# Two transposes of an attention pair in one PSUM tile of two banks, split by one instruction each; value products with one bank

## The chip, the cores and the metric

The kernel runs on one core of a Trainium2 chip. The metric is the device time of one execution in microseconds (us). The engines are TensorE (PE; its weight loads are listed as PEld), VectorE (DVE), ScalarE (ACT), GpSimd (POOL) and SyncE (SP, which here issues DMA). TensorE writes its results into PSUM, eight banks of 512 fp32 values in each partition; ScalarE and VectorE read them from there.

## The reference

Attention whose K and V are averaged over groups of 8 positions feeds two layers of experts. `setup_inputs` multiplies q and k by 8.

```python
# q, k, v: (8, 8, 576, 64) fp32; Sp = 72
k_p = k.reshape(B, H, Sp, 8, D).mean(axis=3)
v_p = v.reshape(B, H, Sp, 8, D).mean(axis=3)
scores = scale * np.matmul(q, k_p.transpose(0, 1, 3, 2))
attn = softmax(scores)                      # over the 72 pooled positions
x = np.matmul(attn, v_p)                    # -> (4608 tokens, 512)
h = np.maximum(np.maximum(x @ w1, x @ w2), x @ w3)      # (4608, 768)
x = h @ w_out                               # (4608, 512)
h = np.maximum(x @ w_in, 0.0)               # (4608, 2048)
out = h * h @ w_out2                        # (4608, 512)
```

## The kernel before

Every fp32 operand of a large product is split in two parts, a high one in the format fp32r and the rest, and a product is three matmuls (high·high, high·low, low·high; `PARTS`). The 4608 tokens are cut into 12 blocks j of `T1` = 384. For each block, attention makes x (512 features as four tiles of 128, one for each pair p of heads), and `moe1(j)` takes x through 18 products with w1, w2, w3 (L528, tile `ps`, evacuated by ScalarE or, as a running maximum `hm`, by VectorE at L536) and four with w_out (L547). The last layer, `moe2`, uses combinations of blocks of its operands and begins at 753 us. Its weights are prepared during the first stage.

`attend` makes the six steps of one pair in one piece of a block; a piece lies within one batch and has n = 384 or 192 tokens. `load` issues K (`kr`, 128x576), q (`qr`) and V (`vr`, 72x1024) on SyncE's queue. `prepare` sums K over groups of 8 on VectorE (L240, `ks`) and writes the scaled result on ScalarE (`kbd`). `softmax` sums V (L247, `vs`), splits it (`vst`), and makes scores (L362, tile `sc`), row maxima (L364, `st`), exponentials (L367), sums and reciprocals (L371, L372), and on GpSimd the normalisation (`ss`). From j = 2 on, `carry` copies the result by DMA into the format that a faster transpose takes (`ssr`). `transpose` turns each head's part on TensorE (L395, `tr`), and ScalarE and VectorE split it (L399 and L400, `pt`). `values` multiplies by V (L424, L425, `av`), joins the two halves of the head (L427 on ScalarE, L428 on VectorE, tile `xf`), and splits the joined tile into x (L134 on ScalarE, L135 on VectorE). Batch 0 is handled "whole": its weights are not split, and its V is pooled by a matmul.

64 pairs of a piece and a pair of heads are computed: 8 whole, 56 split, of these 28 with n = 384 and 28 with 192.

A `kr` buffer and a `vr` buffer are handed out by `place`, by turns: first from four places that the raw weights use too, and after the last weight of w_out has been asked for, from two, so that the loads of K then follow one another in one place and those of V in the other. Raw weights of 8 bytes an element come as `wraw` on SyncE, are rebuilt as fp32 by ScalarE (L161, L162) and VectorE (L163, L166, `wbits`), and split into `w` by ScalarE (L134) and GpSimd (L135).

Every step enters a list with a due time and is emitted in that order; the framework's scheduler then orders the instructions of each engine by its own model of their times. PSUM holds three banks for `ps`, two for `sc`, one for `tr` and two for `av0` and `av1`; the transpose of the second head borrows `av1`.

Of the kernel before, what the change touches and what calls it, by code (L numbers as in the profile page):

```python
# [10 lines left out]
F32 = mybir.dt.float32  # L11
F32R = mybir.dt.float32r
I32 = mybir.dt.int32
U32 = mybir.dt.uint32
AF = mybir.ActivationFunctionType
ALU = mybir.AluOpType
# [4 lines left out]
P = 128  # L21
B, H, S, D = 8, 8, 576, 64
POOL = 8
SP = S // POOL
# [9 lines left out]
T1 = 384  # L34
# [50 lines left out]
def as_f32(ap):  # L85
    return ap.bitcast(F32)
# [8 lines left out]
def attention_moe_kernel(ctx: ExitStack, tc: tile.TileContext, q, k, v, vn, w1, w2, w3, wo1, wi2, wo2, out):  # L95
    nc = tc.nc
# [6 lines left out]
    ident = const.tile([P, P], F32R, name="ident")  # L103
# [4 lines left out]
    for sign, base in ((1, POOL * MID), (-1, POOL - 1 - POOL * MID)):  # L108
        nc.gpsimd.affine_select(
            out=sums, in_=sums, compare_op=ALU.is_ge, fill=0.0, base=base,  # L110
# [22 lines left out]
    def split_to(hi, lo, src, engine):  # L133
        nc.scalar.activation(hi, src, AF.Copy)  # L134
        engine.tensor_tensor(out=lo, in0=src, in1=as_f32(hi), op=ALU.subtract)  # L135

    def split(hl, src, engine=nc.vector):

        split_to(hl[:, 0], hl[:, 1], src, engine)
# [53 lines left out]
    tr_ps = s_at.enter_context(tc.tile_pool(name="tr_ps", bufs=1, space=PSUM))  # L193
    av_ps = s_at.enter_context(tc.tile_pool(name="av_ps", bufs=1, space=PSUM))
# [93 lines left out]
    def score_tiles(n):  # L288
        m = P if n % P == 0 else n // 2
        return [(c, m) for c in range(0, n, m)]  # L290
# [37 lines left out]
    def attend(j, b, s0, n, p, t):  # L328

        kr, vr, qr, pt, sms = [], [], [], [], []  # L330
        first, whole, carried = s0 == 0, b < NATURAL, j >= CARRIED
# [19 lines left out]
        tiles = score_tiles(n)  # L351
        m = tiles[0][1]
# [29 lines left out]
            sms[0] = ssr  # L382

        def transpose():
            if whole:
                pt.append(pt_p.tile([SP, 2, T1], F32, tag="pt", name="pt"))
            else:
                pt.append(pt_p.tile([SP, 2, 2, T1], F32R, tag="pt", name="pt"))
            for h in range(2):
                if h:  # L390
                    tr = av_ps.tile([P, T1], F32R if carried else F32, tag="av1", name="tr")[:SP, :n]
                else:
                    tr = tr_ps.tile([SP, T1], F32R if carried else F32, tag="tr", name="tr")[:, :n]
                for i, (c, _) in enumerate(tiles):
                    nc.tensor.transpose(tr[:, c : c + m], sms[0][:, i, h], (ident if carried else as_f32(ident))[:m, :m])  # L395
                tr = as_f32(tr) if carried else tr
                if not whole:
                    hi, lo = pt[0][:, 0, h, :n], pt[0][:, 1, h, :n]
                    nc.scalar.activation(hi, tr, AF.Copy)  # L399
                    nc.vector.tensor_tensor(out=lo, in0=tr, in1=as_f32(hi), op=ALU.subtract)  # L400
                elif h:
                    nc.vector.tensor_copy(pt[0][:, h, :n], tr)
                else:
                    nc.scalar.activation(pt[0][:, h, :n], tr, AF.Copy)

        def values():
            if t == 0:
                x_t[j][p] = x_p.tile([P, 2, T1], F32R, tag="x", name="x")
            x = x_t[j][p][:, :, t : t + n]
            if whole:  # L410
                av = av_ps.tile([P, T1], F32, tag="av0", name="av0")[:, :n]
                for h in range(2):
                    nc.tensor.matmul(
                        av, lhsT=vst_f[p // 2][:, p % 2, h : h + 2].rearrange("p a d -> p (a d)"), rhs=pt[0][:, h, :n],
                        start=(h == 0), stop=(h == 1),
                    )
                split(x, av)
                return
            hi, lo = pt[0][:, 0, :, :n], pt[0][:, 1, :, :n]
            xf = xf_p.tile([P, T1], F32, tag="xf", name="xf")[:, :n]  # L420
            for h in range(2):
                av = av_ps.tile([P, T1], F32, tag=f"av{h}", name=f"av{h}")[:, :n]
                lhsT = vst[:, p, 2 * h : 2 * h + 2].rearrange("p a d -> p (a d)")
                nc.tensor.matmul(av, lhsT=lhsT, rhs=hi[:, h], start=True, stop=False)  # L424
                nc.tensor.matmul(av, lhsT=lhsT, rhs=lo[:, h], start=False, stop=True)  # L425
                r, o = slice(h * D, (h + 1) * D), slice((1 - h) * D, (2 - h) * D)
                nc.scalar.activation(xf[r], av[o], AF.Copy)  # L427
                nc.vector.tensor_tensor(out=xf[r], in0=av[r], in1=xf[r], op=ALU.add)  # L428
            split(x, xf)

        return load, prepare, softmax, carry, transpose, values

    w1_t, wo1_t = {}, {}
# [395 lines left out]
    for j in range(NB2):  # L829
        for gr in range(NG):  # L830
            more = j + 1 < NB2
            c = moe2_in(j, gr)
# [55 lines left out]
```

## Time and profile before

| | before |
|---|---|
| median of three runs | 1465.66 us (1464.34 to 1467.58) |
| profiled execution | 1463.68 us |
| its span, first to last instruction | 1462.0 us |
| busy: PE, DVE, ACT, POOL | 1426.7, 983.3, 762.5, 177.5 us |
| mean granted TensorE clock | 0.993 of full |

The time of an execution holds the span and about 1.7 us around it. Busy time is the time in which an engine ran an instruction; consecutive instructions of an engine can overlap a little in the records.

### The profile page before, as it was taken

The page shows a single profiled execution, that of the slowest core. Times are in us where ns is not written, and L with a number is a line of the kernel's source. Part 1 is how long each engine was busy: PE and PEld are TensorE (multiplying, and loading weights), DVE is VectorE, ACT ScalarE, POOL GpSimd, SP SyncE. Part 2 cuts the span into 40 slices and gives each one's busy share as a digit, 9 for nine tenths or more (in the row PEclk, how much of TensorE's full clock was granted, in tenths as well). Part 3 has the DMA queues.
Part 4 walks back from the last instruction along what each step waited for, and adds up shares of the span by engine and source line. Part 5 has one row for each costly group of instructions (what it writes and reads, how often), then busy time and mean ns, then how long its engine had stood idle before and what let it go on. Part 6 is the DMA issues. An engine that isn't in the chain of part 4 may idle for free.

```text
span 1462.0 us, 27667 instructions
## 1 busy us (share of the span) xinstructions
PE 1426.7 (98%) x10410; PEld 1401.6 (96%) x10410; DVE 983.3 (67%) x1778; ACT 762.5 (52%) x1983; POOL 177.5 (12%) x229
## 2 busy tenths in 40 slices
PE   6889999999999999999999999999999999999998
PEld 4879999999999999999999999999999999999998
DVE  5896476766765856756336768686766768686775
ACT  7795366664666656654323545363534445454443
POOL 3441022311312212221000000000000000000000
PEclk9999999999999999999999999999999999999999
DMA  7654145543455544432549857666567665665746
GB/s 226 188 164 140 62 145 181 173 137 130 145 170 187 151 145 144 127 123 86 187 162 356 280 176 240 220 208 217 214 231 230 229 212 213 205 238 179 277 139 229
DMA packets 125029, 272.81 MB, mean 187 GB/s; under 512 B 13504, under 2 KB 69568, under 8 KB 124896
## 3 DMA queue, kind: packets, MB, share of 16 engines
q1 hardware_dynamic: 117984, 261.61, 53.4%
q10 hardware_dynamic: 6912, 9.44, 1.8%
q8 instruction: 82, 1.34, 0.4%
q14 instruction: 51, 0.42, 0.1%
HBM read 213.91 MB, written 48.23 MB: 179 GB/s over the span
## 4 chain that ended last, share of the span: by engine, by line
PE 89%; DMA 6%; ACT 3%; DVE 2%; issue 1%; SPq 0%; POOL 0%; DVEq 0%; ACTq 0%; POOLq 0%
PE ps L528 29%; PE ps L688 23%; PE ps L547 10%; PE accB L812 6%; PE accA L812 6%; PE accF L812 3%; DMA wo2s<-wo_dram 3%; PE accE L812 3%; PE accD L812 2%; PE sc L362 2%; ACT ss L367 1%; PE tr L395 1%; PE av L425 1%; PE av L424 1%; DMA kq<-in_k_dram 1%
## 5 line engine op out<-in xcount | busy, mean ns | idle before, releaser
L528 PE MATMUL ps<-x,w 128*128 128x384 f32 x2592 | 493.8, 341 | 5.3 <-ACT w L134 2.7
L528 PEld LDWEIGHTS ps<-x,w 128*128 128x128 f32 x2592 | 449.6, 189 | 8.5 <-ACT w L134 3.0
L688 PE MATMUL ps<-y,wi2s 128*128 128x256 f32 x3024 | 371.5, 277 | 0.5 <-DVE c L659 0.2
L688 PEld LDWEIGHTS ps<-y,wi2s 128*128 128x128 f32 x3024 | 356.6, 188 | 1.5 <-DVE a L659 0.7
L547 PE MATMUL ps<-h,wo 128*128 128x384 f32 x864 | 162.2, 339 | 0.1
L547 PEld LDWEIGHTS ps<-h,wo 128*128 128x128 f32 x864 | 149.2, 188 | 0.7 <-POOL wo L135 0.4
L701 ACT ACTIVATE c<-c 128x512 f32<-128x512 f32 x90 | 56.3, 627 | 169.7 <-DVE c L659 169.1
L659 DVE TENSOR_TENSOR c<-ps,c 128x512 f32<-128x512 f32 x144 | 98.2, 687 | 67.3 <-PE ps L688 64.4
L536 DVE TENSOR_TENSOR hm<-ps,hm 128x384 f32<-128x384 f32 x144 | 79.6, 552 | 76.6 <-PE ps L528 73.6
L134 ACT ACTIVATE g<-c 128x512 fp32r<-128x512 f32 x144 | 90.3, 627 | 56.9 <-DVE c L698 23.3
L812 PE MATMUL accA<-wo2s,g 128*128 128x256 f32 x864 | 115.7, 277 | 0.0
L812 PE MATMUL accB<-wo2s,g 128*128 128x256 f32 x864 | 111.1, 277 | 4.5 <-DMA wo2s<-wo_dram 3.5
L812 PEld LDWEIGHTS accB<-wo2s,g 128*128 128x128 f32 x864 | 104.0, 188 | 5.7 <-issue 1.9
L135 DVE TENSOR_TENSOR g<-c,g 128x512 fp32r<-128x512 f32 x144 | 97.8, 685 | 16.5 <-ACT g L134 16.4
L812 PEld LDWEIGHTS accA<-wo2s,g 128*128 128x128 f32 x864 | 107.1, 188 | 0.0
L367 ACT ACTIVATE ss<-sc,st 128x72 f32<-128x72 f32 (+1 forms) x320 | 98.0, 321 | 15.0 <-DVE st L364 12.0
L373 POOL TENSOR_TENSOR ss<-ss,st 128x432 f32<-128x432 f32 (+1 forms) x64 | 53.7, 839 | 238.8 <-DVE st L372 96.4
L400 DVE TENSOR_TENSOR pt<-tr,pt 72x192 fp32r<-72x192 f32 (+1 forms) x112 | 48.8, 448 | 46.5 <-ACT pt L399 44.9
L427 ACT ACTIVATE xf<-av 64x192 f32<-64x192 f32 (+1 forms) x112 | 45.4, 405 | 58.8 <-PE av L425 47.5
L428 DVE TENSOR_TENSOR xf<-av,xf 64x192 f32<-64x192 f32 (+1 forms) x112 | 50.8, 453 | 36.7 <-ACT xf L427 34.8
L134 ACT ACTIVATE h<-hm 128x384 fp32r<-128x384 f32 x72 | 37.6, 522 | 57.1 <-DVE hm L536 56.4
L367 ACT ACTIVATION_READ_ACCUMULATOR ss<-sc,st 128x1 f32 (+1 forms) x320 | 66.3, 207 | 0.0
(107 smaller groups left out, 1936.5 us busy)
## 6 DMA issues: line engine op xcount, KB each, us to landing
wo2s<-wo_dram SPq DMA_DIRECT2D x252, 512.0 KB
wi2s<-wi_dram SPq DMA_DIRECT2D x24, 512.0 KB
wraw<-in_wo_dram SPq DMA_DIRECT2D x22, 512.0 KB
wraw<-in_w_dram SPq DMA_DIRECT2D x18, 512.0 KB
y_dram<-ys ACTq DMA_DIRECT2D x48, 192.0 KB
wraw<-in_wi_dram SPq DMA_DIRECT2D x16, 512.0 KB
wi_dram<-wraw SPq DMA_DIRECT2D x16, 512.0 KB
wo_dram<-wraw SPq DMA_DIRECT2D x64, 128.0 KB
```

The source lines that it names most:

```text
L134: nc.scalar.activation(hi, src, AF.Copy)
L135: engine.tensor_tensor(out=lo, in0=src, in1=as_f32(hi), op=ALU.subtract)
L367: nc.scalar.activation(ss[:, i, h], src[:, i, h], AF.Exp, bias=st[:, 0, i, h : h + 1], accum_out=st[:, 1, i, h : h + 1],)
L373: nc.gpsimd.tensor_tensor(out=ss, in0=ss, in1=st[:, 2].rearrange("p g (h o) -> p g h o", o=1).to_broadcast([m, g, 2, SP]), op=ALU.mult,)
L428: nc.vector.tensor_tensor(out=xf[r], in0=av[r], in1=xf[r], op=ALU.add)
L528: nc.tensor.matmul(ps, lhsT=w1_t[f, e][:, a, kk * P : (kk + 1) * P], rhs=x[kk][:, c], start=(n == 0), stop=(n == 3 * KD - 1),)
L536: nc.vector.tensor_tensor(out=hm, in0=ps, in1=hm, op=ALU.max)
L547: nc.tensor.matmul(ps, lhsT=wo1_t[kk][:, a, d * P : (d + 1) * P], rhs=hs[kk][:, c], start=(n == 0), stop=(n == 3 * KF1 - 1),)
L659: nc.vector.tensor_tensor(out=out, in0=in0, in1=in1, op=ALU.add)
L688: nc.tensor.matmul(bank[:, u * HT : (u + 1) * HT], lhsT=wi2_t[2 * gr + u][i][:, a, o + kk * P : o + (kk + 1) * P], rhs=y_t[j][m][:, c, kk] ...
L701: nc.scalar.activation(c, c, AF.Relu)
L812: nc.tensor.matmul(bank[:, i * 256 : (i + 1) * 256], lhsT=g[:, a, u * HT + i * P : u * HT + (i + 1) * P], rhs=w[:, u, c], start=(n == 0 an ...
```

## The change

Both heads are transposed into one tile of two banks, one bank for each head, and the tile is split by one ScalarE and one VectorE instruction for the two heads (in `split_to`, so at L134 and L135). The bank that this takes comes from the value products: they have one bank instead of two. For n = 192 the two heads use different halves of it. The transpose of the second head no longer borrows a value bank.

```diff
         def transpose():
+            kind = F32R if carried else F32
+            tr = tr_ps.tile([SP, 2, 512], kind, tag="tr", name="tr")[:, :, :n]
+            for h in range(2):
+                for i, (c, _) in enumerate(tiles):
+                    nc.tensor.transpose(
+                        tr[:, h, c : c + m], sms[0][:, i, h], (ident if carried else as_f32(ident))[:m, :m]
+                    )
+            tr = as_f32(tr) if carried else tr
             if whole:
                 pt.append(pt_p.tile([SP, 2, T1], F32, tag="pt", name="pt"))
+                nc.scalar.activation(pt[0][:, 0, :n], tr[:, 0], AF.Copy)
+                nc.vector.tensor_copy(pt[0][:, 1, :n], tr[:, 1])
             else:
                 pt.append(pt_p.tile([SP, 2, 2, T1], F32R, tag="pt", name="pt"))
-            for h in range(2):
-                if h:
-                    tr = av_ps.tile([P, T1], F32R if carried else F32, tag="av1", name="tr")[:SP, :n]
-                else:
-                    tr = tr_ps.tile([SP, T1], F32R if carried else F32, tag="tr", name="tr")[:, :n]
-                for i, (c, _) in enumerate(tiles):
-                    nc.tensor.transpose(tr[:, c : c + m], sms[0][:, i, h], (ident if carried else as_f32(ident))[:m, :m])
-                tr = as_f32(tr) if carried else tr
-                if not whole:
-                    hi, lo = pt[0][:, 0, h, :n], pt[0][:, 1, h, :n]
-                    nc.scalar.activation(hi, tr, AF.Copy)
-                    nc.vector.tensor_tensor(out=lo, in0=tr, in1=as_f32(hi), op=ALU.subtract)
-                elif h:
-                    nc.vector.tensor_copy(pt[0][:, h, :n], tr)
-                else:
-                    nc.scalar.activation(pt[0][:, h, :n], tr, AF.Copy)
+                split_to(pt[0][:, 0, :, :n], pt[0][:, 1, :, :n], tr, nc.vector)
...
-                av = av_ps.tile([P, T1], F32, tag="av0", name="av0")[:, :n]
+                av = av_ps.tile([P, 512], F32, tag="av", name="av")[:, :n]
...
+            both = av_ps.tile([P, 512], F32, tag="av", name="av") if 2 * n <= 512 else None
             for h in range(2):
-                av = av_ps.tile([P, T1], F32, tag=f"av{h}", name=f"av{h}")[:, :n]
+                if both is None:
+                    av = av_ps.tile([P, 512], F32, tag="av", name="av")[:, :n]
+                else:
+                    av = both[:, h * n : (h + 1) * n]
```

The scheduler puts other instructions in another order too, most in the first 130 us. On VectorE, at the place where x of the last pair of block 1 is finished, the order before reads as follows; the first row is that x, the ks and vs behind it belong to the K and V of batch 2:

```order
L135 TENSOR_TENSOR x<-xf,x 128x192
L166 SCALAR_TENSOR_TENSOR wbits<-wraw,wbits 128x512
L247 TENSOR_REDUCE vs<-vr 72x128
L400 TENSOR_TENSOR pt<-tr,pt 72x384
L163 SCALAR_TENSOR_TENSOR wbits<-wbits,wraw 128x512
L428 TENSOR_TENSOR xf<-av_1460,xf 64x384
L536 TENSOR_TENSOR hm<-ps,hm 128x384
L240 TENSOR_REDUCE ks<-kr 128x72
L400 TENSOR_TENSOR pt<-tr,pt 72x384
L166 SCALAR_TENSOR_TENSOR wbits<-wraw,wbits 128x512
```

The same place on VectorE after the change, line numbers shifted by one (L427 is the old L428); the x of the last pair is the third row from the end:

```order
L247 TENSOR_REDUCE vs<-vr 72x128
L364 TENSOR_REDUCE st<-sc 128x6
L240 TENSOR_REDUCE ks<-kr 128x72
L427 TENSOR_TENSOR xf<-av,xf 64x192
L371 TENSOR_SCALAR st<-st 128x6
L372 RECIPROCAL st<-st 128x6
L240 TENSOR_REDUCE ks<-kr 128x72
L427 TENSOR_TENSOR xf<-av,xf 64x192
L135 TENSOR_TENSOR pt<-tr,pt 72x768
L135 TENSOR_TENSOR x<-xf,x 128x192
L240 TENSOR_REDUCE ks<-kr 128x72
L364 TENSOR_REDUCE st<-sc 128x6
```

Two vs and three ks (one of each stands a little ahead of the rows shown) have moved ahead of the x of the last pair; the last wbits rows, which stood behind it, stand ahead of it too.

On TensorE the order after the change reads as follows between two blocks, about a fifth of the way through the program; av is the value bank, and the rows of 192 and of 384 columns belong to two pieces:

```order
L362 MATMUL sc<-kbd,qr 128x144 x3
L423 MATMUL av<-pt,vst 128x192
L424 MATMUL av<-pt,vst 128x192
L362 MATMUL sc<-kbd,qr 128x144 x3
L423 MATMUL av<-pt,vst 128x384
L424 MATMUL av<-pt,vst 128x384
L389 MATMUL tr<-ident,ssr 72x128 x6
L362 MATMUL sc<-kbd,qr 128x144 x3
```

The transposes of both heads stand together in one row of six, where before they stood in two rows of three, and only three score matmuls stand here between one use of the value bank and the next.

## Rows read from the trace of the kernel before

**Rows 1.** The page, part 1: busy us, share of the span, instructions.

```profile
PE 1426.7 (98%) x10410; PEld 1401.6 (96%) x10410; DVE 983.3 (67%) x1778; ACT 762.5 (52%) x1983; POOL 177.5 (12%) x229
```

**Rows 2.** Stretches: length, busy us (instructions) of each engine, clock, DMA share, GB/s.

```profile
0.00:20.00 20.00, 12.69 (x49) 7.17 (x50) 6.96 (x14) 10.39 (x47) 4.65 (x15) 1.00 0.79 256
20.00:40.00 20.00, 14.72 (x69) 11.59 (x66) 16.17 (x32) 18.09 (x71) 8.33 (x7) 0.83 0.64 185
...
80.00:100.00 20.00, 16.95 (x93) 15.64 (x92) 18.59 (x35) 18.63 (x66) 9.71 (x8) 0.93 0.53 164
100.00:150.00 50.00, 49.05 (x288) 48.08 (x288) 35.18 (x63) 28.42 (x82) 11.47 (x10) 0.97 0.42 123
150.00:200.00 50.00, 50.00 (x303) 49.82 (x302) 23.72 (x44) 21.17 (x61) 4.24 (x8) 1.00 0.26 82
```

**Rows 3.** TensorE's timeline: start, duration, operation, [idle before it <- releaser].

```profile
98.73 0.63 PE L528 MATMUL ps<-x,w 128*128 128x384 f32 x2 [1.88 <-ACT w L134]
...
110.09 0.97 PE L528 MATMUL ps<-x,w 128*128 128x384 f32 x4 [0.85 <-DVE x L135]
```

**Rows 4.** Groups by shape, pt: count, busy us, mean ns, idle before.

```profile
L399 ACT ACTIVATE pt<-tr 72x384 fp32r<-72x384 f32 x56 | 25.5, 481 | 12.2 <-PE tr L395 11.5 <-ACT ys L553 0.4
...
L399 ACT ACTIVATE pt<-tr 72x192 fp32r<-72x192 f32 x56 | 17.4, 320 | 7.8 <-PE tr L395 7.2 <-ACT pt L399 0.4
...
L400 DVE TENSOR_TENSOR pt<-tr,pt 72x384 fp32r<-72x384 f32 x56 | 29.8, 548 | 37.9 <-ACT pt L399 37.1
...
L400 DVE TENSOR_TENSOR pt<-tr,pt 72x192 fp32r<-72x192 f32 x56 | 19.1, 349 | 8.6 <-ACT pt L399 7.8
```

**Rows 5.** TensorE's timeline, 157 to 180 us.

```profile
157.93 0.53 PE L395 MATMUL tr<-ident,ssr 128*72 128x128 f32 x6
158.29 2.33 PE L528 MATMUL ps<-x,w 128*128 128x384 f32 x12
...
163.60 10.28 PE L547 MATMUL ps<-h,wo 128*128 128x384 f32 x58
...
178.66 0.90 PE L362 MATMUL sc<-kbd,qr 128*128 128x144 f32 x6
```

**Rows 6.** Groups by shape, xf, 384 columns.

```profile
L427 ACT ACTIVATE xf<-av 64x384 f32<-64x384 f32 x56 | 27.2, 486 | 29.7 <-PE av L425 28.4
...
L428 DVE TENSOR_TENSOR xf<-av,xf 64x384 f32<-64x384 f32 x56 | 31.0, 553 | 18.1 <-ACT xf L427 17.1
```

**Rows 7.** TensorE's timeline between two blocks.

```profile
302.12 0.41 PE L424 MATMUL av<-pt,vst 72*128 72x384 f32 x1 [0.48 <-DVE pt L400]
```

**Rows 8.** VectorE's timeline, 109 to 132 us.

```profile
109.09 0.68 DVE L166 SCALAR_TENSOR_TENSOR wbits<-wraw,wbits 128x512 int32<-128x512 int32 x1
109.69 0.34 DVE L135 TENSOR_TENSOR x<-xf,x 128x192 fp32r<-128x192 f32 x1
...
115.79 1.22 DVE L247 TENSOR_REDUCE vs<-vr 72x128 f32<-72x1024 f32 x1 [0.20 <-DMA vr<-in_v_dram]
...
122.01 0.75 DVE L240 TENSOR_REDUCE ks<-kr 128x72 f32<-128x576 f32 x1 [1.99 <-DMA kr<-in_k_dram]
...
131.59 0.75 DVE L240 TENSOR_REDUCE ks<-kr 128x72 f32<-128x576 f32 x1 [3.13 <-DMA kr<-in_k_dram]
```

**Rows 9.** SyncE's DMA queue, timeline: time of issue.

```profile
111.79 0.32 SPq L235 DMA_DIRECT2D vr<-in_v_dram  x1
...
118.33 0.34 SPq L230 DMA_DIRECT2D kr<-in_k_dram  x1
```

**Rows 10.** Groups by shape, VectorE reductions.

```profile
L247 DVE TENSOR_REDUCE vs<-vr 72x128 f32<-72x1024 f32 x28 | 33.9, 1211 | 4.2 <-DMA vr<-in_v_dram 3.9
...
L240 DVE TENSOR_REDUCE ks<-kr 128x72 f32<-128x576 f32 x28 | 20.8, 744 | 12.1 <-DMA kr<-in_k_dram 10.0 <-ACT kbd L243 1.8
...
L364 DVE TENSOR_REDUCE st<-sc 128x6 f32<-128x432 f32 x32 | 19.1, 598 | 13.5 <-PE sc L362 13.3
```

**Rows 11.** VectorE's timeline, a wait for a weight conversion.

```profile
102.78 1.35 DVE L163 SCALAR_TENSOR_TENSOR wbits<-wbits,wraw 128x512 int32<-128x512 int32 x1 [1.76 <-ACT wbits L161]
```

## The prediction

> **What bounds the kernel now.** I read the page first. TensorE is busy for 98% of the span, VectorE for 67%, ScalarE for 52% [rows 1]. So an instruction taken from ScalarE or VectorE is worth nothing by itself; it counts only where TensorE waits for those engines. 1462.0 − 1426.7 leaves 35.3 us in which TensorE does nothing, and the table of stretches says where: it lacks 7.3 us up to 20, 5.3 in 20 to 40, 3.1 in 80 to 100, then 0.95 up to 150, and nothing up to 200 [rows 2]. In the second and third of these stretches VectorE and ScalarE are busy 81 to 93%: the start-up, in which weights are rebuilt, K and V pooled and two blocks of attention run, is the only place where they set the pace. TensorE's own timeline then names the last two gates: 1.88 us at 98.73 for a split weight, 0.85 us at 110.09 for the low half of x of pair 3 of block 1 [rows 3]. From there TensorE's chain has no wait until 299. The profiled execution took 1463.7 us, 2.0 less than the median of the runs; the sum below is made on it and then moved up by 2.0.
>
> **What is removed, and its price.** 56 pairs are split; each loses one ScalarE and one VectorE instruction. Rows price the old ones: ScalarE 320 ns for 192 columns and 481 for 384, VectorE 349 and 548 [rows 4]. Twice 192 columns in one instruction should cost about what 384 cost now, so ScalarE saves 2·320 − 481 = 159 ns and VectorE 2·349 − 548 = 150 ns. For 768 columns I extend the line by 161 and 199 ns per 192 columns: 803 and 946 ns, again 159 and 150 saved. Over 56 pairs this is 8.9 us of ScalarE and 8.4 of VectorE. After 100 us both have 30% or more to spare [rows 2], so of it only the merged pairs ahead of the gates can count: by the order four of 192 columns and two of 384, 0.9 us per engine. On TensorE the transposes are the same number in fewer runs: it changes from one kind of matmul to another 815 times in the program before and 762 after. A run of 12 costs 2.24 − 0.08 of overlap = 2.16 us where 58 cost 10.28, 0.177 each [rows 5], so 12 cost 2.12 and a change of kind about 0.04. 53 × 0.04 = 2.1 us if each change costs it; only 15 of the 53 are on the long runs of products, which gives 0.6. I take 0.8 as gain, between 0 and 2.1.
>
> **What the single value bank adds.** The second head's products must now wait until the first head's xf copy and add have read the bank. That takes one ScalarE and one VectorE row: 486 + 553 ns for 384 columns [rows 6], about 1.1 us with the hand-overs, and less for 192. Counting the order of TensorE after the change, 2 us or more of other matmuls stand between the two heads at all but four of the 56 places; those four, at three block boundaries and in the start-up, have 0, 0.3, 0.3 and 0.9 us (0.3 is three score matmuls, as between the value products in the part of TensorE's order shown). There I put in 0.7, 0.7 and 0.5 less what was lost there before: the first boundary already waits 0.48 for the like, a pt row [rows 7]. Net +1.0, bounded by 0 (the waits replace one another) and 3.4 (three full 1.1).
> The Trainium skill ("PSUM — Partial Sum Buffer", section "PSUM bank collisions raise a hardware error") speaks against the change here: a bank which one engine reads may not be written by another, at other columns either, so that halves of one bank are no two buffers and the 192-column tile "both" gains no overlap over the wider one. By it every one of the 56 pairs pays, and the sum would be rival C's. The order, which shows the wait at 192 columns too, agrees with the rule; what hides it is the work between.
>
> **What moves: VectorE's queue in the start-up.** The two orders are the largest change. VectorE takes its queue in order, and a reduction of K (ks) or V (vs) at its head holds all behind it until the load lands. Loads of kr share one buffer and those of vr another, and SyncE issues one only when the reduction before has read it: kr issued at 118.33 was reduced at 122.01, 3.7 us later; vr 111.79 to 115.79, 4.0 [rows 8, 9]. So two ks with less than 3.7 us of VectorE work between stall. Before, such stalls of 1.99 and 3.13 us stand at 122.01 and 131.59 [rows 8], behind the x of pair 3, and TensorE, with x in hand, does not wait. After, three ks and two vs stand ahead of that x.
> First the work. Ahead of x of pair 3 the order after holds on VectorE 3 ks, 2 vs, 3 wbits and 3 st rows more, and for pt 4 rows of 2 × 192 columns and 2 of 768 in place of 8 of 192 and one of 384. By start-to-start times (a row's duration less the 0.08 by which the next starts early): ks 3·0.67, vs 2·1.13, wbits 3·0.60, st 0.7 (one reduction of 0.52, two short rows), pt 4·0.47 + 2·0.87 − 8·0.27 − 0.47 = 1.0; together 7.8 us [rows 4, 8, 10]. On TensorE the same point stands behind 28 more products, 9 scores and 6 transposes: 28·0.177 + 9·0.11 + 6·0.06 = 6.3 us [rows 5]. The gate had no slack (0.85 us of wait), so this alone is +1.5. At the x of pair 2 it is 7 wbits, a ks, a vs, an h and an hm: +7.0 of VectorE against +2.7 of TensorE, less a slack of about half a us, +3.8, which the later gate contains.
> Then the stalls. In the rows of VectorE's order after, xf, st and a reciprocal stand between the first ks shown and the second, 0.28 + 0.07 + 0.10 = 0.45 us against 3.7: a stall of 3.3. Between the vs shown first and the one before it stand 3.3 us (2 wbits, 2 of 192 columns, a ks and a pt of 768) against 4.0: 0.7. Together +4.0; nothing if the loads come earlier than I think, 5.1 if the first of them waits as well.
> Against it: VectorE waits for ScalarE's conversions before this gate, 1.76 us at 102.78 the longest [rows 11]; with more to do it will find more of them ready. I take back 1.5, of 4.4 that the waits from 70 us on come to.
> Behind the gate the next two ks (1.4 and 1.5 us of work ahead of them since the last, so stalls of 2.3 and 2.2) delay the xf which frees the value bank and the hm which frees a product bank, with 3.5 and 7.7 us of TensorE work as cover against 4.0 and 8.4 of VectorE: +1.4.
>
> **Sum.** 1.5 + 4.0 − 1.5 + 1.4 (start-up) + 1.0 (boundaries) − 0.8 (runs) = +5.6 us, 1469.3 on the profiled execution, 1471 against the median. All terms at their kind ends: 1.5 + 0 − 4.4 + 0 + 0 − 2.1 = −5.0; at the unkind: 1.5 + 5.1 − 0 + 2.5 + 3.4 − 0 = +12.5, with 2.5 for both late hand-overs in full.
>
> **Rivals.** A, no change: the ks stalls are there but land on TensorE work, as those before do, or the loads arrive early; then 1.5 − 1.5 + 1.0 − 0.8 = 0.2: 1465.9. For it speaks that the start-up has many orders of the same length; against it that 0.45 us between two ks cannot hide 3.7. B, faster: the start-up is bound by ScalarE's conversions, not by x. The last split of a weight (1.88 us of wait at 98.73) has about 3 us less of ScalarE work ahead of it in the order after, by my count of its rows; if that gate goes (−1.9), VectorE gains its 0.9 on the x gate, and 0.8 comes from the runs: 1465.7 − 3.6 = 1462. It decides if no ks stall over 1 us falls before x of pair 3. C, the bank: were there no work between the two heads, 56 × 1.1 = 62 us, 1527; the order excludes nearly all of it, and 2 of 56 places more than I count cost 2 us, which the range holds. D, the clock: it was granted at 0.83 of full at 20 to 40 us, where TensorE idled, 0.93 at 80 to 100 and 1.00 at 150 to 200 [rows 2], so mostly at 2.4 GHz with parts at 1.2. New idle near 115 could bring a part of 1.2 GHz there: my guess is 2 to 4 us more, 1473 to 1475.
>
> **How the numbers follow.** Forecast with its waits at 1468.6 to 1476: 0.53. A: 0.20. B: 0.13. D: 0.12. C in a visible size: 0.02. A measurement here tells 0.2%, 2.9 us, from no change. Faster than 1462.7: B, 0.12. Same: A, a little of B and the lower edge of the forecast, 0.24. Slower: 0.64. The range leaves out the last tenth of B and of D: 1461.5 to 1477.5; the forecast's own is 1468 to 1475.
>
> **What would show it.** In the profile after, VectorE idle before L240 for the kr load, 2 to 3 us at a time, between 110 and 130 us; TensorE waiting there for VectorE's x or xf, with its busy time in 100 to 150 down from 49.05 to about 44. 28 pt rows each of about 481 and 803 ns on ScalarE. Waits of under 1 us for xf at three block boundaries. From 150 on the same distances as before. I am wrong if TensorE's start-up idle stays at 20 us (A), if it shrinks (B), or if value products wait for xf at many of the pairs (C).

## The result and the profile after

The change makes the kernel slower: 1483.81 us median of five runs (1479.77 to 1484.51) against 1465.66 (1464.34 to 1468.41), a ratio of 1.0122 with a 95% interval of 1.0108 to 1.0136. The direction was forecast, the size was not: +18 us against +5.6, outside the range. The profiled execution has a span of 1482.0 us, 20.0 more than that of [rows 1].

The page of the changed kernel, part 1:

```profile
PE 1437.1 (97%) x10410; PEld 1408.6 (95%) x10410; DVE 974.8 (66%) x1722; ACT 756.7 (51%) x1927; POOL 180.6 (12%) x229
```

VectorE and ScalarE have 56 instructions fewer each and 8.5 and 5.8 us less to do. TensorE has the same 10410 matmuls. It is idle for 1482.0 − 1437.1 = 44.9 us, 9.6 more than in [rows 1], and busy for 10.4 us more with the same work. In this execution a lower clock accounts for some 9 of these 10.4: its mean went from 0.993 to 0.987 of full, and 0.013·1482 − 0.007·1462 = 9.0. That share holds for this execution alone. The five executions of the changed kernel had mean clocks of 0.987, 0.992, 0.990, 0.993 and 0.991, and the one at 0.993 took 1482.44 us all the same; by their mean of 0.991 the clock would account for some 3 us. What the other executions lost in its place is not shown.

The merged instructions, groups by shape (count, busy us, mean ns, idle before); they answer to [rows 4]:

```profile
L134 ACT ACTIVATE pt<-tr 72x768 fp32r<-72x768 f32 x28 | 22.5, 805 | 10.8 <-PE tr L389 10.4
...
L134 ACT ACTIVATE pt<-tr 72x384 fp32r<-72x384 f32 x28 | 13.6, 484 | 2.3 <-PE tr L389 1.8
...
L135 DVE TENSOR_TENSOR pt<-tr,pt 72x768 fp32r<-72x768 f32 x28 | 26.7, 952 | 29.7 <-ACT pt L134 29.6
...
L135 DVE TENSOR_TENSOR pt<-tr,pt 72x384 fp32r<-72x384 f32 x28 | 15.5, 552 | 2.8 <-ACT pt L134 1.7
```

They cost what was forecast (803 and 481, 946 and 548 ns). The saving is real and lies beside TensorE's work.

To see where the time went I cut both executions at the same pieces of work, by counting the products of `moe1` (L528 and L547 before, L527 and L546 after): the starts of the 433rd, 1081st, 1405th, 1981st, 2269th, 2809th and 3241st. Stretches of the kernel before, columns as in [rows 2]:

```profile
0.00:147.13 147.13, 125.85 (x673) 111.57 (x673) 109.10 (x209) 105.64 (x364) 52.38 (x55) 0.93 0.58 178
147.13:277.27 130.14, 130.14 (x801) 129.10 (x801) 79.90 (x172) 71.37 (x234) 24.43 (x36) 1.00 0.41 132
277.27:346.46 69.19, 68.01 (x419) 66.68 (x419) 46.80 (x94) 42.74 (x146) 16.86 (x24) 1.00 0.50 162
...
462.80:521.09 58.29, 58.29 (x360) 57.86 (x358) 39.98 (x78) 36.44 (x114) 15.92 (x21) 1.00 0.52 168
...
630.36:715.70 85.34, 84.40 (x504) 82.67 (x503) 42.49 (x84) 40.61 (x111) 15.90 (x21) 1.00 0.45 146
```

The same stretches of the changed kernel:

```profile
0.00:157.36 157.36, 130.94 (x685) 113.16 (x686) 109.96 (x205) 107.51 (x368) 54.28 (x56) 0.93 0.54 168
157.36:285.66 128.30, 128.30 (x789) 127.57 (x789) 77.07 (x159) 70.63 (x223) 24.28 (x36) 1.00 0.41 131
285.66:360.80 75.14, 71.47 (x425) 70.01 (x425) 48.46 (x95) 45.19 (x149) 19.21 (x27) 0.95 0.49 158
...
475.54:540.70 65.16, 63.94 (x390) 62.91 (x390) 43.37 (x89) 42.82 (x152) 18.68 (x24) 0.97 0.51 164
...
646.51:734.30 87.79, 85.57 (x508) 84.57 (x508) 44.50 (x86) 42.81 (x112) 16.25 (x21) 0.98 0.43 146
```

The start-up is 10.2 us longer (157.36 against 147.13). The three stretches that hold a change of block with many scores are longer by 5.9, 6.9 and 2.5, and there the clock, 1.00 before, has a mean of 0.95, 0.97 and 0.98. The stretches between are shorter by 1.8, 1.6 and 3.5, in part because some attention work has moved into their neighbours: the three longer ones hold 6, 30 and 4 more matmuls, the start-up 12 more. Up to the 3241st product this adds up to 10.2 + 8.4 = 18.6 us; the last layer adds 1.4.

The 8.4 us are clearer when the part from the 433rd to the 3241st product is taken whole, before and after:

```profile
147.13:715.70 568.57, 566.45 (x3476) 559.69 (x3475) 357.96 (x751) 327.98 (x1053) 125.14 (x174) 1.00 0.46 145
```

```profile
157.36:734.30 576.94, 569.56 (x3464) 563.61 (x3464) 349.90 (x702) 321.49 (x994) 126.29 (x173) 0.99 0.44 143
```

TensorE's idle time there goes from 2.1 to 7.4 us, 5.3 more. The clock stands at half in three places near 313, 494 and 671 us, 13.6 us in all, which costs 6.8. Of these 12.1 only 8.4 show, because TensorE's other work takes 3.7 us less. 12 score matmuls have moved into the start-up (1.3 us at 0.11 each). The remaining 2.4 fit the fewer changes from one kind of matmul to another: counted in TensorE's order there are 363 in this part, 414 before, and 51 of them at the prediction's 0.04 are 2.0.

How a boundary is lost is seen best at 668 us, in three timelines of the changed kernel (start, duration, operation, [idle before it <- releaser]). TensorE:

```profile
668.22 0.35 PE L423 MATMUL av<-pt,vst 72*128 72x192 f32 x1
668.41 0.27 PE L424 MATMUL av<-pt,vst 72*128 72x192 f32 x1
670.90 0.45 PE L423 MATMUL av<-pt,vst 72*128 72x384 f32 x1 [2.22 <-DVE xf L427]
```

ScalarE and VectorE in the same stretch:

```profile
667.80 0.32 ACT L367 ACTIVATE ss<-sc,st 128x72 f32<-128x72 f32 x1
...
669.59 0.35 ACT L367 ACTIVATE ss<-sc,st 128x72 f32<-128x72 f32 x1
...
670.05 0.32 ACT L426 ACTIVATE xf<-av 64x192 f32<-64x192 f32 x1
```

```profile
670.49 0.36 DVE L427 TENSOR_TENSOR xf<-av,xf 64x192 f32<-64x192 f32 x1
```

The products of a pair's second head are written by 668.7, and the first head of the next pair needs their bank. The copy that begins to free the bank stands behind four more exponentials in ScalarE's queue and starts at 670.05; VectorE's add ends at 670.85, and TensorE goes on at 670.90. Two short instructions (0.32 and 0.36) make a hand-over of 2.2 us, because ScalarE takes its queue in order. The Trainium skill says so of these engines ("PSUM — Partial Sum Buffer", section "Engine vs sequencer instructions": their queues are strictly first in, first out); this trace agrees, with 1.4 us for which the copy stood ready. Of the six waits for xf ahead of value products in this execution three are of this kind, from one pair to the next (1.10, 0.56 and 2.22 us); in the other three the second head waits for the first (0.97, 1.11 and 0.27).

At the boundary near 310 us there are three waits of the kind (1.11 and 0.56 for xf, 1.00 for pt), and then the clock falls. TensorE's timeline there, six products before and nine after:

```profile
307.21 1.30 PE L527 MATMUL ps<-x,w 128*128 128x384 f32 x6
...
315.83 3.26 PE L527 MATMUL ps<-x,w 128*128 128x384 f32 x9
```

The nine take 0.36 us each, where the six before took 0.22 with their ends: the granted level went from 2.4 to 1.2 GHz, with the work that follows the waits. Two stretches of the changed kernel at half clock, this one and one in the start-up:

```profile
312.90:319.70 6.80, 5.89 (x24) 5.85 (x25) 3.32 (x9) 3.99 (x22) 1.03 (x2) 0.50 0.17 57
...
111.50:118.30 6.80, 6.19 (x25) 6.14 (x26) 5.26 (x8) 3.04 (x14) 3.11 (x3) 0.50 0.37 108
```

The start-up, TensorE's timeline of the changed kernel from 102 to 125 us:

```profile
102.86 0.35 PE L423 MATMUL av<-pt,vst 72*128 72x192 f32 x1 [1.10 <-DVE xf L427]
...
108.65 0.36 PE L423 MATMUL av<-pt,vst 72*128 72x192 f32 x1 [0.97 <-DVE xf L427]
...
112.11 1.33 PE L546 MATMUL ps<-h,wo 128*128 128x384 f32 x3 [2.45 <-POOL wo L135]
...
123.69 0.44 PE L423 MATMUL av<-pt,vst 72*128 72x384 f32 x1
...
124.78 0.61 PE L527 MATMUL ps<-x,w 128*128 128x384 f32 x2
```

VectorE, same kernel, the K reductions that I had forecast as stalls:

```profile
122.48 0.75 DVE L240 TENSOR_REDUCE ks<-kr 128x72 f32<-128x576 f32 x1 [2.32 <-DMA kr<-in_k_dram]
...
126.16 0.75 DVE L240 TENSOR_REDUCE ks<-kr 128x72 f32<-128x576 f32 x1 [1.28 <-DMA kr<-in_k_dram]
```

The stalls are there. But TensorE is late before them, through hand-overs of the bank and a weight split on GpSimd: it starts the 246th product at 116.70 us, 6.6 later than before, and the first stall begins at 120.16. It reaches the x of pair 3 (124.53 on VectorE, 124.78 on TensorE) without an idle time; from 113 to 129 us its one wait is 0.38 at 119.48, for ScalarE.

### The profile page after: what moved, and what is told of

Its sections match the earlier page's. It is cut to its first block, busy times and chain, and to the rows that moved or that the text cites. A ratio compares the mean times of both kernels' runs of the same rounds, so it can differ in the third digit from the quotient of the medians.

```text
span 1482.0 us, 27649 instructions
## 1 busy us (share of the span) xinstructions
PE 1437.1 (97%) x10410; PEld 1408.6 (95%) x10410; DVE 974.8 (66%) x1722; ACT 756.7 (51%) x1927; POOL 180.6 (12%) x229
## 4 chain that ended last, share of the span: by engine, by line
PE 79%; DMA 10%; DVE 4%; ACT 3%; issue 2%; POOL 1%; SPq 0%; ACTq 0%; POOLq 0%; DVEq 0%
PE ps L527 25%; PE ps L687 21%; PE ps L546 8%; PE accB L811 6%; PE accA L811 6%; DMA wo2s<-wo_dram 5%; PE accE L811 3%; PE accF L811 3%; PE accD L811 2%; PE sc L362 2%; DMA kr<-in_k_dram 1%; ACT ss L367 1%; PE tr L389 1%; PE av L423 1%; DMA wraw<-in_wi_dram 1%
## 5 line engine op out<-in xcount | busy, mean ns | idle before, releaser
L527 PE MATMUL ps<-x,w 128*128 128x384 f32 x2592 | 497.2, 342 | 5.8 <-POOL w L135 1.8
L527 PEld LDWEIGHTS ps<-x,w 128*128 128x128 f32 x2592 | 452.8, 190 | 10.2 <-POOL w L135 2.8
L546 PE MATMUL ps<-h,wo 128*128 128x384 f32 x864 | 162.3, 339 | 3.8 <-POOL wo L135 3.0
L546 PEld LDWEIGHTS ps<-h,wo 128*128 128x128 f32 x864 | 150.2, 189 | 5.3 <-POOL wo L135 3.9
L134 ACT ACTIVATE g<-c 128x512 fp32r<-128x512 f32 x144 | 90.3, 627 | 58.9 <-DVE c L697 23.3
L135 DVE TENSOR_TENSOR g<-c,g 128x512 fp32r<-128x512 f32 x144 | 97.6, 685 | 17.3 <-ACT g L134 17.3
L427 DVE TENSOR_TENSOR xf<-av,xf 64x192 f32<-64x192 f32 (+1 forms) x112 | 50.8, 454 | 59.5 <-ACT xf L426 58.2
L134 ACT ACTIVATE h<-hm 128x384 fp32r<-128x384 f32 x72 | 37.6, 522 | 59.3 <-DVE hm L535 59.1
L135 DVE TENSOR_TENSOR pt<-tr,pt 72x384 fp32r<-72x384 f32 (+1 forms) x56 | 42.1, 752 | 32.6 <-ACT pt L134 31.3
```

What stands on the lines that cost most here:

```text
L527: nc.tensor.matmul(ps, lhsT=w1_t[f, e][:, a, kk * P : (kk + 1) * P], rhs=x[kk][:, c], start=(n == 0), stop=(n == 3 * KD - 1),)
L546: nc.tensor.matmul(ps, lhsT=wo1_t[kk][:, a, d * P : (d + 1) * P], rhs=hs[kk][:, c], start=(n == 0), stop=(n == 3 * KF1 - 1),)
```

## The experiments

The theory "bank" or "hand-over": what costs is that the value products wait for the evacuation of the one bank, the second head's for the first head's and the next pair's for the second head's, behind what stands in the two queues, and the clock behind the waits. Its rivals: "order" (any such change puts the start-up in a worse order) and "K stall", the theory of the prediction. "Late at 432" below is the start of the 433rd product of `moe1` less 147.13, that of the kernel before; "later part" is what is added between it and the 3241st product. Both come from one profiled execution of each kernel. Executions of one kernel differ by several us (19 of the kernel before: 1462.61 to 1470.13), so 2 or 3 us between two such numbers say little. The changed kernel has 10.2 and +8.4.

**Merge without losing a bank** (e1), on the kernel before, for 192 columns alone:

```diff
+            if n <= 256 and not whole:
+                tr = tr_ps.tile([SP, T1], kind, tag="tr", name="tr")[:, : 2 * n].rearrange("s (h n) -> s h n", h=2)
...
+                split_to(pt[0][:, 0, :, :n], pt[0][:, 1, :, :n], tr, nc.vector)
+                return
```

> Merges the two heads' transposes and their split for the 28 pairs of 192 columns alone, into the one transpose bank; the two value banks stay. Theory 'bank' (the single value bank costs the time, through waits for xf and the lower clock behind them): no loss, 1462 to 1467 us. Theory 'order' (any merge puts the start-up in a worse order on VectorE, K and V reductions ahead of x, and that is 8 of the 18 us): 1471 to 1476 us, with TensorE busy for about 43 of the 50 us from 100 to 150.

Measured: 1468.27 us, ratio 1.0009 (0.9993 to 1.0024). Late at 432: 3.1; later part −2.6. That is just above the range of "bank" and well below that of "order". A merge at 192 columns that takes no bank away costs nothing that can be measured, and gains nothing either; the wide pairs were not merged without the loss of a bank. "Order" as stated, that any merge costs 8 us in the start-up, falls.

**One bank without the merge** (e2), on the kernel before:

```diff
-    tr_ps = s_at.enter_context(tc.tile_pool(name="tr_ps", bufs=1, space=PSUM))
+    tr_ps = s_at.enter_context(tc.tile_pool(name="tr_ps", bufs=2, space=PSUM))
...
-                    tr = av_ps.tile([P, T1], F32R if carried else F32, tag="av1", name="tr")[:SP, :n]
+                    tr = tr_ps.tile([SP, T1], F32R if carried else F32, tag="tr", name="tr")[:, :n]
...
+            both = av_ps.tile([P, 512], F32, tag="av", name="av") if 2 * n <= 512 else None
             for h in range(2):
-                av = av_ps.tile([P, T1], F32, tag=f"av{h}", name=f"av{h}")[:, :n]
+                if both is None:
+                    av = av_ps.tile([P, 512], F32, tag="av", name="av")[:, :n]
+                else:
+                    av = both[:, h * n : (h + 1) * n]
```

> Nothing is merged: each head is transposed into a bank of its own, two banks that take turns, and split by its own instructions; the value products have one bank as in the change. Theory 'bank': the whole loss is there without any merge, 1480 to 1486 us, waits of TensorE for xf at block boundaries near 300, 490 and 670 us. Theory 'order' (the merge does the start-up's part): 1472 to 1477 us.

Measured: 1486.24 us, ratio 1.0124 (1.0090 to 1.0157). Late at 432: 12.0; later part +6.2. The whole loss is there with nothing merged, as "bank" said, 0.2 us above its range.

**Products of both heads first** (e3), on the changed kernel:

```diff
+            if both is not None:
+                multiply(0)
+                multiply(1)
             for h in range(2):
+                if both is None:
+                    multiply(h)
...
                 nc.scalar.activation(xf[r], av[o], AF.Copy)
```

> The change, but for 192 columns the products of both heads are written before the first copy out of the bank, so the second head has no wait for the first. Theory 'bank': about half of the hand-overs are gone, 1472 to 1477 us, and the waits for xf in front of 192-column products are gone. Theory 'order': the start-up keeps its loss, and with it 1478 to 1484 us.

Measured: 1469.10 us, ratio 1.0020 (1.0008 to 1.0032). Late at 432: 6.3; later part −4.9. This gives back 15 of the 18 us, more than the 7 to 12 that I expected. TensorE's timeline of this kernel shows the four matmuls of a pair in one go:

```profile
285.08 0.26 PE L425 MATMUL av<-pt,vst 72*128 72x192 f32 x1
285.17 0.27 PE L426 MATMUL av<-pt,vst 72*128 72x192 f32 x1
285.28 0.27 PE L425 MATMUL av<-pt,vst 72*128 72x192 f32 x1
285.39 0.27 PE L426 MATMUL av<-pt,vst 72*128 72x192 f32 x1
```

What TensorE waits for ahead of the value products, from the list of waits (waited for, us in total, times, longest us), of the kernel before, of the changed kernel, of e2 and of e3:

```profile
PE av L424 <- DVE xf L428: 0.9, 1, 0.9
```

```profile
PE av L423 <- DVE xf L427: 6.2, 6, 2.2
```

```profile
PE av L428 <- DVE xf L432: 4.6, 5, 1.8
```

```profile
PE av L425 <- DVE xf L438: 2.1, 4, 0.9
```

The Trainium skill's rule that the prediction cites ("PSUM — Partial Sum Buffer", section "PSUM bank collisions raise a hardware error": no two engines on one bank at once in the same partitions, at other columns either) is kept here by the program's waits: in the traces of the changed kernel and of e3 none of the 224 value products runs while xf reads a value bank, where in the kernel before, with two banks, 20 do. Written first, both halves are done before any reading begins, and the rule costs nothing within a pair; the four waits that e3 has left are from one pair to the next.

**The bank taken from the scores** (e4): the changed kernel with `sc_ps` of one bank and `av_ps` of two.

```diff
-    sc_ps = s_at.enter_context(tc.tile_pool(name="sc_ps", bufs=2, space=PSUM))
+    sc_ps = s_at.enter_context(tc.tile_pool(name="sc_ps", bufs=1, space=PSUM))
...
-    av_ps = s_at.enter_context(tc.tile_pool(name="av_ps", bufs=1, space=PSUM))
+    av_ps = s_at.enter_context(tc.tile_pool(name="av_ps", bufs=2, space=PSUM))
```

> The change with its merged transposes, but the bank is taken from the scores (one instead of two) and the value products keep two. Theory 'bank': the waits for xf are gone; if the scores don't wait in their place, 1462 to 1468 us. Theory 'order': the start-up still loses 8, 1472 us or more. If a bank is needed by whatever loses it, the scores wait for exponentials: above 1475 us.

Measured: 1475.52 us, ratio 1.0055 (1.0033 to 1.0076). Late at 432: 15.0; later part −6.8. The boundaries lose nothing with two value banks, but the start-up loses more than in the change. TensorE's timeline there shows what waits:

```profile
125.23 1.00 PE L362 MATMUL sc<-kbd,qr 128*128 128x144 f32 x6 [1.45 <-ACT ss L367]
...
131.66 0.85 PE L389 MATMUL tr<-ident,ssr 128*72 128x128 f32 x6 [2.88 <-DVE pt L135]
```

That the start-up misses a bank wherever it is taken fits this but is not shown, because the order there changed too.

**Products first in block 1 alone** (e5) and **after block 1 alone** (e6), e3's edit under a condition:

```diff
+            early = both is not None and j == 1      # e5;  j > 1 in e6
+            if early:
+                multiply(0)
+                multiply(1)
```

> The change, with the products of both heads ahead of the first copy for the four 192-column pairs of block 1 alone. Theory 'hand-over' (what costs is that the second head waits for the first head's evacuation, behind whatever stands in ScalarE's and VectorE's queues, at the start-up and at block boundaries alike): the start-up gains about 4 us, the boundaries stay lost, 1478 to 1481 us. Theory 'K stall' (the start-up loses to K reductions that wait ahead of x): nothing gained in the start-up, 1482 to 1485.

> The same for the 192-column pairs after block 1 alone. Theory 'hand-over': the three boundary losses near 300, 490 and 670 us go, the start-up stays 10 us late: 1472 to 1476 us. If the boundaries were lost to another order and not to the hand-over: 1480 us or more.

Measured: e5 1480.44 us, ratio 1.0101 (1.0086 to 1.0115), late at 432 by 7.5, later part +6.2; e6 1471.41 us, just under its range, ratio 1.0035 (1.0021 to 1.0049), late at 432 by 11.2, later part −6.2. Each gives back its own stretch. The four pairs of block 1 are worth 3 to 5 us in the start-up (7.5 against 10.2, and 6.3 in e3 against 11.2 in e6), little more than two profiles can tell apart; the pairs of later blocks are worth 11 to 15.

**Four places for K and V of batch 2** on the changed kernel (e7) and on e3 (e8):

```diff
     def load_k(b, p):
+        shared[0] = b < 3
...
-        shared[0] = kk < KF1 - 1
```

> The change, but the loads of K and V of batch 2 go on taking turns over four places instead of one place each, so that a reduction on VectorE does not wait for a load that the reduction before it held up. Theory 'K stall': the waits of VectorE for kr between 115 and 130 us go and TensorE gets x and the value bank earlier, 1476 to 1479 us. Theory 'hand-over': those waits go too, but TensorE has been held up by 6 us before them, so little changes: 1481 to 1485.

> Products of both heads first at 192 columns, and four places for K and V of batch 2. Here the waits for xf in the start-up are fewer, so that a K stall could show: theory 'K stall' 1461 to 1465 us, below the kernel before; theory 'hand-over': 1467 to 1470, as with the products first alone.

Measured: e7 1490.13 us, ratio 1.0181 (1.0152 to 1.0210), late at 432 by 9.0, later part +14.4; e8 1474.11 us, ratio 1.0061 (1.0043 to 1.0079), late by 7.8, later part +0.3. Both lie above both of their ranges and are slower than the kernels that they were made from, mostly in the later part. There TensorE is idle for 13.5 us in e7, 7.8 of them in seven waits for xf; why there are more of these stays open. The K stalls went, and a wait for V came in their place on VectorE in e7:

```profile
120.34 1.22 DVE L248 TENSOR_REDUCE vs<-vr 72x128 f32<-72x1024 f32 x1 [3.56 <-DMA vr<-in_v_dram]
```

So this did not tell the two theories apart cleanly, which is why the next pair leaves the loads out.

**No loads of K and V of batch 2**, on the changed kernel (e9) and on the kernel before (e10); `load_v` is changed alike:

```diff
     def load_k(b, p):
+        if b == 2:
+            return sums[:, :POOL].rearrange("p (a b) -> p a b", a=1).to_broadcast([P, SP, POOL])
...
```

> The change without the loads of K and V of batch 2: the eight reductions of that batch read a small constant spread over the same shape, so they take as long and wait for no load (K and V of batch 2 are ones in it). Theory 'K stall' (loads that VectorE waits for hold up the start-up): the 13 us that are lost from about 103 to 130 us shrink to 6 or less, 1473 to 1478 us in all. Theory 'hand-over': the start-up stays 10 us late, 1480 to 1484.

> The kernel before without the same loads, as a control: its waits for K of batch 2 stand behind the last x of block 1, and TensorE waits for none of them, so both theories expect 1463 to 1467 us.

Measured: e9 1483.04 us, ratio 1.0113 (1.0092 to 1.0133), late at 432 by 11.6, later part +2.8; e10 1474.20 us, ratio 1.0054 (1.0033 to 1.0076), late by 7.6, later part +0.3. In e9 one stall of 1.44 us for K is left in that stretch, of 4.5 in the change, and the start-up is as late as in the change; what TensorE waits for is:

```profile
102.52 0.36 PE L427 MATMUL av<-pt,vst 72*128 72x192 f32 x1 [1.95 <-DVE xf L431]
...
113.87 1.65 PE L531 MATMUL ps<-x,w 128*128 128x384 f32 x4 [2.89 <-DVE x L135]
```

That is what "hand-over" said. The control was a surprise: with banks as before and less to load, the kernel before loses 7.6 us in the start-up, where TensorE's timeline now shows this:

```profile
114.91 0.37 PE L399 MATMUL tr<-ident,ssr 128*72 128x128 f32 x3 [3.65 <-DMA ssr<-ss]
```

So with both banks in place the start-up can lose 8 us, and e9 alone does not settle "K stall": a gain from the missing loads and a loss like the control's could cancel in it. What speaks against "K stall" is the changed kernel's own timeline above, where TensorE is late before the first stall and hardly waits after it.

**Two value banks, products first, merged at 192 columns** (e11) and **the same unmerged** (e12): e1 and e3 together, with `av_ps` of two buffers of one tag; e12 leaves e1's part out.

```diff
-    av_ps = s_at.enter_context(tc.tile_pool(name="av_ps", bufs=1, space=PSUM))
+    av_ps = s_at.enter_context(tc.tile_pool(name="av_ps", bufs=2, space=PSUM))
...
+            both = av_ps.tile([P, 512], F32, tag="av", name="av") if 2 * n <= 512 else None
```

> Two value banks that take turns and one transpose bank, as many as before; at 192 columns both heads are transposed into that one bank and split by one instruction each, and the products of both heads go into the halves of one value bank ahead of the first copy, so that the next pair has the other. If the merge is worth something once no bank is lost: 1459 to 1464 us, below the kernel before. If the start-up order decides alone: 1464 to 1470.

> The two value banks that take turns, with the products of both heads first at 192 columns, as in the fastest kernel so far, but each head transposed and split by itself as in the kernel before. If the merge of the transposes gives a part of the 4.7 us: 1463 to 1466 us. If all of it comes from the products and the banks: 1460 to 1463 us.

Measured: e11 1461.66 us, ratio 0.9969 (0.9957 to 0.9981), the fastest kernel of the study; late at 432 by 0.4, later part −6.6. e12 1467.39 us, above both of its ranges, ratio 1.0018 (1.0005 to 1.0032); late by 7.1, later part −6.2. After the start-up the two are alike, so the 6 us gained there do not come from the merge. They come with the products of both heads written first, and one bank is enough for that: e3 and e6 have −4.9 and −6.2. The part from the 433rd to the 3241st product in e12:

```profile
154.27:716.65 562.38, 562.33 (x3473) 558.71 (x3473) 354.13 (x754) 328.94 (x1054) 133.05 (x174) 1.00 0.46 148
```

Idle time is 0.1 us where the kernel before has 2.1, and busy time 562.3 where it has 566.4. The 4 us of work fit the changes of kind again, 326 against 414. The two kernels differ mostly in the start-up; that the merge makes its order better is not shown.

**Other orders of the start-up**: one number that sets due times of block 1's attention, in the kernel before and in the changed one.

```diff
-BRISK = 0.7
+BRISK = 0.6      # and 0.66, 0.8
```

> The kernel before with BRISK 0.6 instead of 0.7, which moves due times of block 1's attention and so the start-up's order alone. If the order decides the start-up: 3 to 10 us late at the 432nd product, 1468 to 1475 us. If the bank does: within 3 us of the kernel before, 1463 to 1468.

> The kernel before with BRISK 0.66. If the order decides: 0 to 8 us late, 1465 to 1473 us. If the bank does: 1463 to 1468.

> The kernel before with BRISK 0.8. If the order decides: 3 to 10 us late, 1468 to 1475 us. If the bank does: 1463 to 1468.

> The changed kernel with BRISK 0.6. If the order decides the start-up: anywhere from 0 to 12 us late at the 432nd product, 1473 to 1485 us in all. If the bank does: 9 to 13 us late, 1482 to 1487.

> The changed kernel with BRISK 0.66. If the order decides: 0 to 12 us late at the 432nd product, 1473 to 1485 us. If the bank does: 9 to 13 us late, 1482 to 1487.

> The changed kernel with BRISK 0.8. If the order decides: 0 to 12 us late at the 432nd product, 1473 to 1485 us. If the bank does: 9 to 13 us late, 1482 to 1487.

The ratios to the kernel before are, in the order 0.6, 0.66, 0.8, for the kernel before 1.0043 (1.0014 to 1.0072), 0.9998 (0.9977 to 1.0020) and 1.0045 (1.0029 to 1.0062), for the changed one 1.0083 (1.0065 to 1.0101), 1.0139 (1.0084 to 1.0194) and 1.0118 (1.0065 to 1.0172). With the two kernels at 0.7:

| BRISK | before: us, late at 432, later part | changed: us, late at 432, later part |
|---|---|---|
| 0.6 | 1472.93, 8.2, 0.0 | 1478.89, 8.1, +3.9 |
| 0.66 | 1467.12, −0.8, +0.8 | 1486.70, 10.3, +6.9 |
| 0.7 | 1465.66, 0, 0 | 1483.81, 10.2, +8.4 |
| 0.8 | 1473.28, 7.1, +0.9 | 1483.65, 11.5, +5.0 |
| mean | 1469.7, 3.6, +0.4 | 1483.3, 10.0, +6.0 |

With two banks, 0.6 and 0.8 came out in the range of "order" alone; with one, 0.66 in that of "bank" alone and 0.6 in that of "order" alone. So neither decides the start-up alone. The later part is separate in the two columns in every row. The start-up is 8 to 12 us late with one bank and −1 to 8 late with two: the bank costs 6 on the mean, and the order spreads it so far that at 0.6 there is no difference. Four orders are few, but the other runs agree: of all kernels here that go head by head in block 1, the eight with one value bank are 8.1 to 12.0 late (these four, e2, e6, e7, e9), and the six with two value and two score banks −0.8 to 8.2 (these four, e1, e10). Against the same four orders the change costs 13.5 us; by this sample, the other 4 to 5 of its 18 are that the kernel before had one of the two good orders.

The part from the 433rd to the 3241st product, over all kernels but e7 and e8:

| kernels | TensorE idle, us | lost to the lower clock, us |
|---|---|---|
| one value bank, head by head (the changed kernel, its three BRISK runs, e2, e5, e9) | 6.2 to 7.8 | 0 to 6.8 |
| two value banks, head by head (the kernel before, its three BRISK runs, e1, e4, e10) | 0.5 to 3.5 | 0 |
| products of both heads first (e3, e6, e11, e12) | 0.1 to 0.9 | 0 |

Every kernel with one bank and head-by-head products has the waits; the lower clock behind them varies, and the changed kernel's 6.8 is the most of it.

## Why the prediction was wrong, by its own steps

**The single value bank (+1.0, from 0 to 3.4) is the step that failed.** From the 433rd to the 3241st product TensorE waits 5.3 us more, above the upper end of the term, and the lower clock behind the waits costs 6.8 in the profiled execution. In time that part is +8.4, +6.0 over four orders, and some 6 more are lost in the start-up on the mean. Three things went wrong in the step. I priced a hand-over by its own two rows, 1.1 us [rows 6], and at 670.90 us it took 2.2, since exponentials stood ahead of the copy in ScalarE's queue; I had asked what TensorE has to do meanwhile, and not what ScalarE has to do first. I priced the second head's wait for the first and counted four places; the changed kernel waits six times for xf alone, three of them, with the longest, at the first head of the next pair, and the pt and the x behind a late hand-over wait too (1.00 at 313.81). And I put nothing into this term for the clock behind such waits.

**VectorE's queue in the start-up (+1.5 + 4.0 − 1.5 + 1.4).** The sum of 5.4 was half of the 10.2 that the start-up lost, and its main term was wrong. The forecast stalls for K came: 2.32 us at 122.48 where I had 3.3, then 1.28 and 0.90 where I had 2.3 and 2.2; the 0.7 for V did not. But TensorE had been held up by 6 us of waits between 99 and 113, so the stalls delayed nothing that was ready. The gate was not the x of pair 3. What did hold it up: hand-overs of the bank (1.10, 0.97) and a weight's split that came 2.45 late, none of which is in my sum. The sign that I had named, TensorE's busy time in 100 to 150 us down to about 44, came with 43.12, and by these other waits:

```profile
100.00:150.00 50.00, 43.12 (x237) 40.26 (x238) 31.67 (x55) 26.24 (x82) 12.44 (x9) 0.93 0.41 120
```

So that the direction came out right is luck: 5.4 of the forecast 5.6 stood for a queue that held nothing up. The 1.4 was also wrong in itself, as the numbers beside it give 0.5 + 0.7 = 1.2.

**What is removed (no gain on the path)** was right: the rows cost what I extended them to (VectorE is busy for 8.5 us less where I had 8.4, ScalarE for 5.8 where I had 8.9), and neither engine's relief shows in the time. The gain for fewer runs, 0.8 out of 0 to 2.1, is there and was put too low: 2.4 us after the start-up alone. Its price rests on one run of 12 products (2.24 us) beside two that took 2.33 and 2.31, yet the traces bear 0.04 out: e12 has 88 changes of kind fewer than the kernel before and about 4 us less to do.

**Rivals.** C, the bank at every pair, named the right resource and the wrong size: I gave it 2 in 100 because most places have 2 us of work between. A was right that the stalls land on TensorE's work, and wrong that nothing else is lost. B falls: TensorE was 2.9 us ahead at the 217th product (99.94 against 102.83), which may be B's gain, and 0.1 behind at the 231st. D, the clock, was priced at 2 to 4 us near 115. It was at half from 111.5 to 118.3 us, 3.4 us, but over the whole start-up both kernels have 20.4 us at half clock; what the profiled execution lost more lies at block boundaries, where D did not look.

## What to carry to other kernels

Before a buffer is given up, price its hand-over from the moment at which it is ready to the moment at which it is free, with all that stands ahead of the freeing instruction in its engine's queue at that place, not by the duration of that instruction. Where two outputs share a bank, write both ahead of the first read: that one change of order gave back 15 of 18 us and left TensorE 0.2 us of idle time from the 433rd to the 3241st product. With both banks kept it came to 0.3% below the kernel before together with the merge at 192 columns, and to 0.2% above it without, a difference that lies mostly in the start-up. Runs of one kind of matmul count too: some 0.04 us for each change of kind that goes. And where a scheduler orders a crowded start-up, nudge one due time in both versions before a difference of a few us is put down to an edit.

## What the runs showed that was not expected

A wait of 1 to 2 us in the midst of a busy stretch can cost as much again in clock, and need not: after 3.7 us of waits between 306 and 314 us nine products took 3.26 us, and the longest hand-over of the changed kernel, 2.22 us at 670.90, was followed by three and six products at half clock:

```profile
671.51 1.33 PE L527 MATMUL ps<-x,w 128*128 128x384 f32 x3
...
673.27 1.92 PE L527 MATMUL ps<-x,w 128*128 128x384 f32 x6
```

In e9 the same hand-over has the same wait, and the same products run at full clock:

```profile
667.95 0.45 PE L427 MATMUL av<-pt,vst 72*128 72x384 f32 x1 [2.22 <-DVE xf L431]
...
668.55 0.79 PE L531 MATMUL ps<-x,w 128*128 128x384 f32 x3
...
669.69 1.27 PE L531 MATMUL ps<-x,w 128*128 128x384 f32 x6
```

Why the clock fell behind one and not behind the other stays open. In the start-up of the unchanged layout, orders that differ by one due-time factor lie up to 9 us apart, and taking loads away made the kernel slower by 8.
